# A gated linear attention with an MLP behind it: results kept in 20 buffers and stored by SP, five input buffers, and a new plan

## The chip, the core and the metric

The kernel runs on one core of a Trainium2 chip. The core has five engines that work side by side and wait for each other by semaphores: TensorE (PE in the profile; PEld is its weight load), VectorE (DVE), ScalarE (ACT), GpSimd (POOL) and SyncE (SP). Here SP only issues DMA transfers: loads, transposes and some stores. POOL computes and issues DMA too. Matrix products are written to PSUM, which the kernel uses as six banks and one larger buffer for scores; everything else lies in SBUF.

The metric is the device time of one execution in microseconds, the median of several runs. The difference that can be told from none is about 0.2%.

## What is computed

For 4 batches, 8 heads, 768 steps and head size 48, a state of 48 x 48 per head is decayed by a gate and updated by an outer product; the query reads it. The result, 3072 rows of 384, goes through two matrices with SiLU between them.

```python
f = 1.0 / (1.0 + np.exp(-f_logit))
for t in range(S):
    state = f[:, :, t, :, None] * state + np.einsum('bhd,bhe->bhde', k[:, :, t], v[:, :, t])
    y[:, :, t] = np.einsum('bhd,bhde->bhe', q[:, :, t], state)
...
x = np.ascontiguousarray(attn_out.transpose(0, 2, 1, 3)).reshape(B * S, H * D)
h = x @ w_in                     # 384 -> 2048
g = h * (1.0 / (1.0 + np.exp(-h)))
return (g @ w_out).astype(np.float32)   # 2048 -> 384
```

## The kernel before

The 768 steps are cut into 6 chunks of 128; with 4 batches that makes 24 units. Unit u is chunk u // 4 of batch u % 4, and units 2P and 2P+1 form pair P. Four tiles `f`, `k`, `q`, `v` (128 x 384 in f32) are loaded for each unit.

A unit goes through these tasks, in the names of the planner (`make_tasks`, from L72) and the lines of `emit` (from L467) that carry them out:

- E, L (ACT, L463 and L465): the logarithm of the gate, by exponential and logarithm, for one unit or for a pair at once.
- cs (PE, L511 and L515): its cumulative sum over the chunk. ia, al, a (ACT, L518, L522, L520): exponentials of that sum.
- ki, vb (POOL, L524 and L526): k scaled, v cast to bf16. qg (DVE, L528): q scaled.
- The scaled q and k are transposed, either by PE and a copy (tq L534, qkc L536), or, for the units in `turned`, by one DMA transpose that SP issues (qkD, L538).
- sc (PE, L545): scores. at (DVE, L549): the causal mask. y (PE, L554 and L558): the unit's result. yc (DVE, L562): its copy to bf16.
- d (PE, L576), sd (DVE, L581 or L583), su (POOL, L587): the new state, used by the same batch's next unit, u + 4.
- The result is transposed for the first matrix, by PE and a copy (yT L568, xc L570), or, for the units in `turned_y`, by a DMA transpose (xD, L564).

Then, for each pair (for the first four pairs unit by unit), come mi (PE, L492: products with w_in), si (ACT, L488: SiLU), mo (PE, L502: products with w_out, four tasks for each unit), oc (DVE, L505: the unit's 128 x 384 result to SBUF, tile `o`) and so (L508: its store). A store is issued by POOL, or by SP for units from `late_store` on. The weights come in four parts each: wi (L475) and wo (L478), issued by POOL. On ACT exponentials and SiLU need different function sets, so that a change between them costs a table load (L615).

What runs when is settled before the kernel is emitted. `schedule` (from L196) plays the tasks through with assumed durations and gives each engine the ready task of lowest priority value: `pace` x unit + `rank` of its kind + small offsets. `rel` holds a task back to an earliest time. `keep_*` and `hold_*` rule when ACT changes its function set. Where PE would be idle early on, it adds filler products (L480). The tasks are then emitted in the order of the starts found; that order is each engine's program and, for SP, the order of its one DMA queue. Only the order carries over to the chip: real waits are by semaphores.

`SLOTS` (L47) gives the number of buffers of each kind, and the playing-through decides which task gets which. A task that needs a buffer waits until its last user is done. `f`, `k`, `q`, `v` have six buffers, each for a pair of units, so loads can run 12 units ahead; `o` has four.

PE's order before, at three places that matter below (mi_u_j: unit or pair and part; mo_u_m: unit and part):

```
... sc_3 mi_0_1 mi_1_1 mi_2_1 y_3 d_3 yT_3 mi_0_3 mi_1_3 mi_2_3 mi_3_1 mi_3_3 mi_0_0 mi_1_0 mi_2_0 tq_4 mi_3_0 sc_4 mi_0_2 ...
... y_21 mo_18_0 mo_18_1 mo_18_2 mo_18_3 mo_19_0 mo_19_1 mo_19_2 mi_20.21_0 ...
... y_22 mo_19_3 y_23 mo_20_0 ... mo_21_2 mi_22.23_0 ... mi_22.23_7 mo_21_3 mo_22_0 ... mo_23_3
```

Of the kernel before, what the change touches and what calls it, by code (L numbers as in the profile page):

```python
# [20 lines left out]
PAIRS = UNITS // 2  # L21
NTILES = 16
CFG = dict(
    turned=(11, 12, 13, 14, 15, 16, 17, 18, 19, 20, 21, 22, 23),
    turned_y=(7, 10, 12, 14, 15, 17, 19, 20, 21, 22, 23),
    paired=(),
    single_logs=3,
    single=4,
    late_store=18,
    rank=dict(ldf=-74.11, ldk=306.83, ldq=178.45, ldv=335.15, E=-327.79, cs=2020.94, ia=-759.0, ki=-2046.16, vb=759.95,  # L30
         qg=-1495.72, tq=-1801.69, qkc=-1166.67, sc=-2328.29, at=2478.3, y=-12.62, yc=-690.3, yT=-3037.0, xc=1416.83,
         d=2253.93, sd=-1035.38, su=1438.09, qkD=-1636.38, xD=-2535.0, wi=-1290.0, wo=1188.34, mi=-71.8, si=-1785.07,
         mo=3071.62, oc=5435.06, so=-1357.98),
    extra={},
    rel={"wi_0": 23.54, "wi_1": 17.61, "wi_2": 27.48, "wi_3": 20.24, "wo_0": 29.34, "wo_1": 34.31, "wo_2": 38.63, "wo_3":
         39.74},
    pace=166.65,
    mstep=4.83,
    keep_exp=3000.87,
    keep_silu=2633.26,  # L40
    hold_exp=1.01,
    hold_silu=1.0,
    margin=0.0,
    dm=0.16,
)

SLOTS = dict(f=6, k=6, q=6, v=6, e=2, lf=3, ia=2, qk=5, vb=6, qkT=4, atm=3, yb=3, xT=4, hT=4, sd=2, al=6, o=4,  # L47
             st0=1, st1=1, st2=1, st3=1, bank=6, sc=1)


# [339 lines left out]
def planned(cfg, slots):  # L390

    tasks, T = make_tasks(cfg)
    warm = schedule(tasks, slots, cfg)
    return sorted(tasks + warm, key=lambda t: (t.start, t.idx))
# [3 lines left out]
def kernel(  # L398
# [32 lines left out]
    buf = {}  # L431
    for cls, n in SLOTS.items():
        for s in range(n):
# [12 lines left out]

    tasks = planned(CFG, SLOTS)
    where = {}
# [148 lines left out]
    with tc.manual_schedule():  # L597
# [7 lines left out]
        for cls in ("lf", "qk"):  # L605
            for s in range(SLOTS[cls]):
                nc.vector.memset(buf[cls, s][:, :, :, D:64], 0.0)
# [38 lines left out]
```

## Time and profile before

| | before |
|---|---|
| median of 3 runs | 186.0 us (185.97 to 186.32) |
| the profiled execution | 186.71 us, span of its instructions 184.8 us |
| mean granted TensorE clock | 0.981 |
| busy: PE, ACT, DVE, POOL | 175.7, 126.6, 90.9, 72.2 us |
| stores: by POOL, by SP | 18, 6 of 192 KB each |
| issue to landing, median: POOL's stores, SP's stores | 3.7 us, 1.9 us |
| loads f, k, q, v | 24 each, 192 KB, landing after 3.9 to 4.2 us |

The span runs from the first instruction to the last. A duration from the timeline is one of that execution, so sums are made against its span. Two pages' parts are read together below: what an engine waited for, and the chain that ended last, which goes back from the last instruction to what released each step. Matrix products overlap, so the duration of one product is longer than what it adds to PE's time; the chain's pieces show what it adds.

### The profile page before, as it was taken

To read this page: it belongs to the slowest core of one execution; us is meant where nothing else is said; L and a number is where in the kernel's file an instruction comes from. 1 tells how busy PE (TensorE), PEld (TensorE's weight loads), DVE (VectorE), ACT (ScalarE), POOL (GpSimd) and SP (SyncE) were. 2 spreads that over 40 slices of the span, in tenths; PEclk is the share of its full clock that TensorE was granted. 3 is DMA by queue.
4 is the path that set the end of the run, shared out by engine and by line. 5 is a ranking of instruction groups with operands and counts; after the bars stand their busy time and mean duration, and the time that the engine had idled before them with its cause. 6 is when DMAs were issued, how large, how long until landed. Compare 5 with 4: busy or idle time off the path is not lost.

```text
span 184.8 us, 4961 instructions
## 1 busy us (share of the span) xinstructions
PE 175.7 (95%) x1999; PEld 134.2 (73%) x1999; DVE 90.9 (49%) x178; ACT 126.6 (69%) x216; POOL 72.2 (39%) x122
## 2 busy tenths in 40 slices
PE   7985997999999999999999999999999999999992
PEld 5764777888668787878687678587587776776860
DVE  4185871241476558764914954545365156171021
ACT  5954476554853999899899479698789679550910
POOL 2335648117049418281940853614733616000000
PEclk9998599999999999999999999999999999999999
DMA  6997999999999908999799999799898895704012
GB/s 125 221 208 149 182 224 220 201 175 147 201 198 290 193 21 165 240 199 188 145 178 227 235 174 230 149 228 229 153 242 174 170 212 120 156 4 128 0 44 83
DMA packets 123893, 31.53 MB, mean 171 GB/s; under 512 B 118656, under 2 KB 123008, under 8 KB 123872
## 3 DMA queue, kind: packets, MB, share of 16 engines
q1 hardware_dynamic: 119008, 24.55, 71.6%
q0 software_dynamic: 4864, 6.69, 16.3%
q8 instruction: 15, 0.25, 0.6%
q14 instruction: 6, 0.05, 0.1%
HBM read 25.17 MB, written 4.72 MB: 162 GB/s over the span
## 4 chain that ended last, share of the span: by engine, by line
PE 78%; DMA 7%; SPq 5%; POOL 4%; issue 3%; DVE 0%; POOLq 0%; DVEq 0%
PE bank L502 34%; PE bank L492 31%; SPq L456 5%; DMA w_in_sb<-in_moe_w_in_dram 4%; PE sc L545 3%; DMA k<-in_k_dram 3%; PE bank L558 2%; PE bank L554 2%; PE bank L511 2%; POOL st L587 2%; PE bank L576 2%; PE bank L534 1%; POOL w_in_sb L475 1%; POOL qk L524 1%; PE bank L568 1%
## 5 line engine op out<-in xcount | busy, mean ns | idle before, releaser
L488 ACT ACTIVATE hT<-bank 128x512 bf16<-128x512 f32 x96 | 55.1, 601 | 30.1 <-PE bank L492 27.1
L492 PE MATMUL bank<-xT,w_in_sb 128*128 128x128 bf16 (+1 forms) x768 | 68.9, 246 | 1.1 <-DMA w_in_sb<-in_moe_w_in_dram 0.9
L502 PE MATMUL bank<-w_out_sb,hT 128*128 128x384 bf16 x384 | 69.0, 326 | 0.0
L492 PEld LDWEIGHTS <-w_in_sb 128*128 128x128 bf16 x768 | 58.6, 98 | 8.2 <-DMA w_in_sb<-in_moe_w_in_dram 1.4
L502 PEld LDWEIGHTS <-hT 128*128 128x128 bf16 x384 | 35.5, 98 | 20.4
L549 DVE TENSOR_TENSOR atm<-sc,triu 128x512 bf16<-128x512 f32 x48 | 30.9, 686 | 27.6 <-PE sc L545 27.6
L587 POOL TENSOR_TENSOR st<-sd,al 48x192 bf16<-48x192 f32 x40 | 20.0, 501 | 35.0 <-DVE sd L581 28.5
L524 POOL TENSOR_TENSOR qk<-k,ia 128x384 bf16<-128x384 f32 x24 | 23.8, 999 | 15.3 <-DMA k<-in_k_dram 6.9
L615 ACT ACT_TABLE_LOAD x21 | 26.9, 1283 | 0.4
L505 DVE COPY o<-bank 128x384 f32<-128x384 f32 x24 | 13.3, 555 | 19.6 <-PE bank L502 15.0
L508 POOL DMA_DIRECT2D out_dram<-o x18 | 10.3, 571 | 25.2 <-DVE o L505 25.1
L562 DVE CAST yb<-bank 128x384 bf16<-128x384 f32 x24 | 13.2, 554 | 12.2 <-PE bank L558 7.8
L518 ACT ACTIVATE ia<-bank 128x384 f32<-128x384 f32 x24 | 11.2, 491 | 10.8 <-PE bank L515 6.6
L528 DVE TENSOR_TENSOR qk<-q,bank 128x384 bf16<-128x384 f32 x24 | 13.1, 551 | 11.1 <-ACT bank L520 9.3
L536 DVE COPY qkT<-bank 128x1024 bf16<-128x1024 bf16 x11 | 7.6, 690 | 17.1 <-PE bank L534 17.0
L526 POOL CAST vb<-v 128x384 bf16<-128x384 f32 x24 | 12.1, 506 | 8.5 <-DMA v<-in_v_dram 8.4
L480 PE MATMUL bank<-idle 128*128 128x256 bf16 x72 | 13.4, 339 | 1.1 <-DVE idle L599 1.1
L463 ACT ACTIVATE e<-f 128x768 f32<-128x768 f32 (+1 forms) x15 | 10.7, 713 | 4.1 <-DMA f<-in_f_logit_dram 4.0
L520 ACT ACTIVATE bank<-bank 128x384 f32<-128x384 f32 x24 | 11.6, 489 | 0.3
L545 PE MATMUL sc<-qkT 48*128 48x128 bf16 x192 | 9.8, 222 | 1.4 <-DVE qkT L536 1.3
L465 ACT ACTIVATE lf<-e 128x768 bf16<-128x768 f32 (+1 forms) x15 | 10.7, 716 | 0.4
L545 PEld LDWEIGHTS <-qkT 48*128 48x128 bf16 x192 | 5.5, 95 | 6.4 <-issue 3.7
(35 smaller groups left out, 119.4 us busy)
## 6 DMA issues: line engine op xcount, KB each, us to landing
f<-in_f_logit_dram SPq DMA_DIRECT2D x24, 192.0 KB, 4.0
q<-in_q_dram SPq DMA_DIRECT2D x24, 192.0 KB, 3.9
k<-in_k_dram SPq DMA_DIRECT2D x24, 192.0 KB, 4.2
v<-in_v_dram SPq DMA_DIRECT2D x24, 192.0 KB, 4.1
out_dram<-o POOLq DMA_DIRECT2D x18, 192.0 KB, 3.7
w_in_sb<-in_moe_w_in_dram POOLq DMA_DIRECT2D x4, 384.0 KB, 6.5
w_out_sb<-in_moe_w_out_dram POOLq DMA_DIRECT2D x4, 384.0 KB, 8.6
out_dram<-o SPq DMA_DIRECT2D x6, 192.0 KB, 1.9
```

Of the source, the lines that this page charges most:

```text
L480: return nc.tensor.matmul(at("warm", rest[0])[:, 0:256], idle[:, 0:128], idle, start=True, stop=True)
L488: return nc.scalar.activation(at("hT", P)[:, per * j:per * (j + 1), lo:hi], h, AF.Silu)
L492: nc.tensor.matmul(h[:, i, :], w_in_sb[:, kk, n * 128:(n + 1) * 128], at("xT", P)[:, kk, lo:hi], start=(kk == 0), stop=(kk == KT - 1))
L502: nc.tensor.matmul(o, at("hT", P)[:, n, i * C:(i + 1) * C], w_out_sb[:, n, :], start=(n == 0), stop=(n == NT - 1))
L505: nc.vector.tensor_copy(at("ob", u), at("o", u)[:, 0:d_model])
L524: nc.gpsimd.tensor_mul(at("qk", u)[:, 1, :, 0:D], at("k", P)[:, i], at("ia", u))
L528: nc.vector.tensor_mul(at("qk", u)[:, 0, :, 0:D], at("q", P)[:, i], at("cs", u)[:, 0:HD].rearrange("p (h d) -> p h d", d=D))
L545: nc.tensor.matmul(a_ps[:, r, p, :], qkT[lo:lo + D, 1, p, :], qkT[lo:lo + D, 0, p, :], start=True, stop=True)
L549: nc.vector.tensor_mul(at("atm", u)[:, r], at("sc", u)[:, r], triu[:, None, :].to_broadcast([C, NP, C]))
L562: nc.vector.tensor_copy(at("yb", u), at("y", u)[:, 0:HD])
L587: nc.gpsimd.tensor_mul(at("st", u)[lo:lo + D, :, r * D:(r + 1) * D], at("sd", u)[lo:lo + D, :, r * D:(r + 1) * D], at("al", u)[lo:lo + D, ...
L615: nc.scalar.preload_act_table_set(tables[turn[id(t)]])
```

## The change

The numbers of the planner are replaced, among them which units are transposed by DMA. `late_store=0` gives all 24 stores to SP, and `rel` now names an earliest time for the stores of units 0 to 17. `SLOTS` takes one buffer each from `f`, `k`, `q`, `v` and gives `o` 20 buffers for four. The code that emits the tasks is the same, two lines further down.

```diff
--- before.py
+++ after.py
@@ -21,30 +21,32 @@
 PAIRS = UNITS // 2
 NTILES = 16
 CFG = dict(
-    turned=(11, 12, 13, 14, 15, 16, 17, 18, 19, 20, 21, 22, 23),
-    turned_y=(7, 10, 12, 14, 15, 17, 19, 20, 21, 22, 23),
+    turned=(8, 10, 11, 12, 13, 14, 15, 16, 17, 18, 19, 20, 21, 22, 23),
+    turned_y=(7, 10, 11, 12, 13, 14, 16, 17, 18, 19, 20, 21, 22, 23),
     paired=(),
     single_logs=3,
     single=4,
-    late_store=18,
-    rank=dict(ldf=-74.11, ldk=306.83, ldq=178.45, ldv=335.15, E=-327.79, cs=2020.94, ia=-759.0, ki=-2046.16, vb=759.95,
-         qg=-1495.72, tq=-1801.69, qkc=-1166.67, sc=-2328.29, at=2478.3, y=-12.62, yc=-690.3, yT=-3037.0, xc=1416.83,
-         d=2253.93, sd=-1035.38, su=1438.09, qkD=-1636.38, xD=-2535.0, wi=-1290.0, wo=1188.34, mi=-71.8, si=-1785.07,
-         mo=3071.62, oc=5435.06, so=-1357.98),
+    late_store=0,
+    rank=dict(ldf=-274.93, ldk=-6.43, ldq=-41.44, ldv=84.54, E=-487.94, cs=661.52, ia=25.69, ki=-923.11, vb=746.88,
+         qg=-1254.96, tq=-717.13, qkc=-1681.18, sc=-760.61, at=2386.54, y=201.04, yc=-903.01, yT=-753.16, xc=2561.22,
+         d=816.17, sd=-1700.33, su=-952.45, qkD=-1345.7, xD=-1132.08, wi=808.99, wo=2162.98, mi=187.68, si=-172.94,
+         mo=2099.98, oc=4900.92, so=2468.15),
     extra={},
-    rel={"wi_0": 23.54, "wi_1": 17.61, "wi_2": 27.48, "wi_3": 20.24, "wo_0": 29.34, "wo_1": 34.31, "wo_2": 38.63, "wo_3":
-         39.74},
-    pace=166.65,
-    mstep=4.83,
-    keep_exp=3000.87,
-    keep_silu=2633.26,
-    hold_exp=1.01,
-    hold_silu=1.0,
-    margin=0.0,
-    dm=0.16,
+    rel={"wi_0": 18.84, "wi_1": 18.77, "wi_2": 27.73, "wi_3": 17.67, "wo_0": 28.08, "wo_1": 27.82, "wo_2": 38.93, "wo_3":
+         41.06, "so_0": 154.46, "so_1": 169.69, "so_2": 173.54, "so_3": 134.53, "so_4": 134.8, "so_5": 177.21, "so_6":
+         174.72, "so_7": 167.9, "so_8": 169.39, "so_9": 147.12, "so_10": 123.29, "so_11": 156.38, "so_12": 152.75, "so_13":
+         152.0, "so_14": 161.31, "so_15": 162.52, "so_16": 131.89, "so_17": 155.6},
+    pace=129.78,
+    mstep=6.0,
+    keep_exp=3697.77,
+    keep_silu=3881.14,
+    hold_exp=0.51,
+    hold_silu=0.83,
+    margin=0.01,
+    dm=0.19,
 )
 
-SLOTS = dict(f=6, k=6, q=6, v=6, e=2, lf=3, ia=2, qk=5, vb=6, qkT=4, atm=3, yb=3, xT=4, hT=4, sd=2, al=6, o=4,
+SLOTS = dict(f=5, k=5, q=5, v=5, e=2, lf=3, ia=2, qk=5, vb=6, qkT=4, atm=3, yb=3, xT=4, hT=4, sd=2, al=6, o=20,
              st0=1, st1=1, st2=1, st3=1, bank=6, sc=1)
```

The orders that this gives, where the working speaks of them. POOL early on, before and after (wi_n, wo_n: parts of the weights):

```
before: ki_2 vb_2 wi_1 su_1 ki_3 wi_3 vb_3 su_2 wi_0 su_3 wi_2 wo_0 ki_4 vb_4 wo_1 su_4 wo_2 wo_3 ki_5 ...
after:  ki_2 vb_2 wi_3 su_1 ki_3 wi_0 wi_1 su_2 vb_3 su_3 wi_2 wo_0 wo_1 ki_4 vb_4 su_4 wo_2 wo_3 ki_5 ...
```

PE after, at the same three places as above:

```
... sc_3 mi_0_3 mi_1_3 mi_2_3 y_3 d_3 mi_0_0 yT_3 mi_1_0 mi_2_0 mi_3_0 mi_3_3 mi_0_1 mi_1_1 mi_2_1 tq_4 mi_3_1 sc_4 mi_0_2 ...
... y_20 y_21 mo_17_3 mo_18_0 mo_18_1 mo_18_2 mo_18_3 mo_19_0 sc_22 mo_19_1 mo_19_2 mi_20.21_0 ...
... y_22 y_23 mo_19_3 mo_20_0 ... mo_21_2 mi_22.23_0 ... mi_22.23_7 mo_21_3 mo_22_0 ... mo_23_3
```

SP's queue in the last stage (so_u: a store):

```
before: q_22 qkD_21 k_22 v_22 q_23 k_23 v_23 xD_20 xD_21 qkD_22 so_18 qkD_23 xD_22 xD_23 so_19 ... so_23
after:  q_22 k_22 so_3 v_22 q_23 k_23 v_23 qkD_22 so_4 xD_20 xD_21 qkD_23 so_9 so_10 so_0 so_12 so_13 so_11
        so_16 so_17 so_18 xD_22 xD_23 so_14 so_15 so_19 so_20 so_7 so_8 so_1 so_21 so_2 so_6 so_22 so_5 so_23
```

## The prediction

> **What bounds the kernel now.** I read the share of busy time first, then what PE waited for, then PE's busy time by stretch, and last the chain that ended last and the queues around its weak places.
>
> What PE waited for (engine, line, tile, releaser: total us, times, longest):
>
> ```profile
> PE bank L534 <- POOL qk L524: 1.3, 1, 1.3
> PE sc L545 <- DVE qkT L536: 1.3, 2, 1.1
> PE bank L492 <- DMA w_in_sb<-in_moe_w_in_dram: 0.9, 1, 0.9
> PE bank L568 <- DVE yb L562: 0.5, 1, 0.5
> ```
>
> Busy time of the engines in two long stretches (start:end, length, then busy us and instructions of PE, PEld, DVE, ACT, POOL, then granted clock, DMA share, GB/s):
>
> ```profile
> 60.00:84.00 24.00, 24.00 (x335) 19.16 (x333) 16.16 (x30) 22.59 (x35) 11.45 (x19) 1.00 0.80 158
> 108.00:132.00 24.00, 24.00 (x244) 17.98 (x242) 11.57 (x22) 20.61 (x35) 11.26 (x19) 1.00 1.08 197
> ```
>
> All waits of PE together are some 5 us, all before 36.4 us. From there to the last product at 181.26 us PE never waits, at full granted clock. So there are three terms: when PE becomes dense (36.41 us), the PE work after that (144.85 us), and the tail of 3.5 us to the span's 184.8. What is saved on POOL, DVE, ACT or DMA is worth nothing unless one of these moves.
>
> What makes PE dense at 36.41, in POOL's part of the timeline (start, us; first three lines) and in the chain that ended last (last two):
>
> ```profile
> 22.36 0.81 POOL L475 DMA_DIRECT2D w_in_sb<-in_moe_w_in_dram  x1
> 24.68 0.80 POOL L475 DMA_DIRECT2D w_in_sb<-in_moe_w_in_dram  x1
> 29.27 0.80 POOL L475 DMA_DIRECT2D w_in_sb<-in_moe_w_in_dram  x1
> ...
> 29.27 7.09 DMA w_in_sb<-in_moe_w_in_dram
> 36.41 2.85 PE bank L492 x48
> ```
>
> The four parts of w_in come one by one; the second to fourth issue at the times shown. PE waits 0.94 us for the third (to 32.40), and the fourth, landing at 36.36, starts the dense run.
>
> **The change, part by part.**
>
> PE work. `turned` gains units 8 and 10, so two tasks tq (eight transposes each) leave PE. `turned_y` gains 11, 13, 16 and 18 and loses 15: three tasks yT fewer. Prices from the dense part of the chain:
>
> ```profile
> 55.66 0.17 PE bank L568 x3
> ...
> 71.23 0.45 PE bank L534 x8
> ```
>
> 2 x 0.45 + 3 x 0.17 = 1.41 us less. Nothing covers it, because PE is the bound: −1.41. The products of L492 and L502, of scores, y and d keep their number and shapes; one filler more (73 for 72) lies before the dense run. On DVE two copies L536 (0.69 us) and three L570 (0.35) go too, worth nothing. ACT loses two table loads (19 changes of function set for 21, 1.28 us each), also off the path.
>
> Head. In POOL's new order the second and third parts of w_in follow each other directly, ahead of su_2 and vb_3; the fourth stays behind su_3. So the third issues at about 22.36 + 0.81 = 23.17 instead of 24.68: 1.5 us earlier. The third and fourth landed 36.36 − 32.40 = 4.0 us apart although issued 4.6 apart, which looks like one queue served in turn; then the fourth can land up to 1.5 us earlier too (29.27 + 5.3, the shortest landing of w_in, is 34.6). PE can get back only its own waits there, 0.94 + 0.18 + 0.13 = 1.25 us. The other end: the DMA share in this stretch is 1.2, saturated, so the fourth may land as before: 0. I take −0.9, nearer the gain, since no byte is added and the third is simply asked for earlier. vb_3 moves behind two issues and su_2, to about 25.6 us; y_3 needs it at 26.75, so 1.1 us of cover; if gone, it delays su_3 and the fourth part by as much.
>
> Stores. Eighteen issues leave POOL (0.57 us each, 10.3 us busy, plus the 25.1 us that POOL waited there for results). POOL is busy 39% of the span and PE waits for it nowhere after 36 us: 0. SP now issues all 24, at 0.33 us when the queue is clear. None stands before the last loads, so the saturated DMA (share about 1.0 from 72 to 150 us) carries 18 x 192 KB less while loads run. A gain only if a load was late: 0.
>
> Five input buffers. A load of unit u waits until unit u−10 has been read, instead of u−12. In the trace E of units 16 and 17 starts at 102.32 us, released by its load of 98.64: loads run at most some five units ahead mid-span, less than ten. Early on, unit 10's first load would wait for an exponential that ended long before (at 5.2 us). Cost 0.
>
> More transposes by DMA. SP carries 29 for 24, each 1.2 to 1.3 us to issue, landing 3.5 us (qkT) or 2.6 us (xT) later. Covers in PE's order, summed with the durations above: from a unit's cumulative sum to its scores, for units transposed by DMA, at least 9.5 us after against 8.4 before; from y to its first L492 product, at least 5.0 against 4.55. The old minima ran without a wait. Between: if a transpose lands at its slowest (5.7 us for 3.5) and the cover is used up, 2.2 us each. I take 0, bounds 0 and 4.4 (two such).
>
> Last stage. SP before, from 156 us:
>
> ```profile
> 156.15 1.23 SPq L538 DMA_TRANSPOSE qkT<-qk  x1
> 157.47 0.53 SPq L508 DMA_DIRECT2D out_dram<-o  x1
> 158.09 1.28 SPq L538 DMA_TRANSPOSE qkT<-qk  x1
> 165.28 2.79 SPq L564 DMA_TRANSPOSE xT<-yb  x2
> 168.12 14.14 SPq L508 DMA_DIRECT2D out_dram<-o  x5
> ```
>
> Nine stores now stand between the transposes of unit 23's scores and of unit 22's y, in a gap where SP idled from 159.4 to 165.3. In the new order PE has 11.85 us of work from the end of y_21 to the end of y_23; qkD_23 leaves SP 3.3 us into it and xD_22 is wanted at 12.2, so the nine fit if each takes under 0.99 us. Measured: 0.33 to 0.57 us on SP, and 0.13 x 15 / 3 = 0.65 us of all DMA engines for the last three. Cost 0. The remaining stores lie under 16 us of PE work after that; only so_5 stands between so_22 and the last one, issued about 2 us ahead of it, so the tail keeps its 3.5 us (bounds 0 and +0.65, one store in the way).
>
> Sum: 184.8 − 1.41 − 0.9 = 182.5 of span. The profiled run took 186.71 and the median of the runs is 186.0, 1.2 above the span; so 183.7 us.
>
> The Trainium skill, DMA: Bandwidth & Descriptors, section "Issuing engines are not separate DMA queues", says that issuing from several engines saves only sequencer time, since all share the same DMA engines. By it moving stores to SP brings nothing and costs SP's time, which is how they stand in the sum.
>
> **The rivals.**
>
> Slower, the last stage: in one queue the nine stores hold up xD_22 and xD_23, and the products of units 22 and 23, which start right behind (170.16), wait. For: loads on the same queue took 0.7 to 3 us each while DMA was full. Against: the share there was 0.1 to 0.7. At 1.5 us a store PE idles 9 x (1.5 − 0.99) = 4.6 us: 188.3. It turns the sign from 0.99 + 2.3/9 = 1.25 us a store. The Trainium skill, DMA: Bandwidth & Descriptors, "Queues, rings and completion order", has each DMA engine take one ring's descriptors in order and alternate between rings; by it the stores, formerly on POOL's ring, now precede the transposes. No row shows that collision.
>
> Slower or same, SP mid-span: it issues in order, and a transpose whose input is late holds the loads behind it. xD_7 already kept SP idle from 61.5 to 67.9. One score transpose at 5.7 us with its cover gone gives back 2.2: 185.9; two, 188.1. Against: the covers counted above.
>
> Head not moved, because the weights share a full DMA: only the 1.41 counts, 184.6.
>
> Same, the clock: granted 0.50 from 18 to 24 us, after idle gaps at 13.4 to 17.5. If the new fillers leave it low for 3.4 us more (half the time from 18 to 24, rounded up), the first products lose 1.7: 186.0 − 1.41 + 1.7 = 186.3. The Trainium skill, TensorE: Matmul & The Clock Gate, "What's actually happening", names a free-running window of 3.4 us; the 6 us here agree roughly with two.
>
> **How the numbers follow.** Forecast 0.57 (own range 182.6 to 185.2), head not moved 0.13, clock 0.06, last stage 0.09, SP mid-span 0.15 (0.03 of it within). A measurement here tells 0.2%, 0.37 us, from no change. Faster 0.70, same 0.09, slower 0.21. The range 182.6 to 187.2 leaves out 0.04 below, and above it the last stage with the worse third of SP mid-span, 0.14.
>
> **What would show it.** Right: L534 with 72 and L568 with 30 products; PE dense from about 35.5 us; no wait of PE after; the last product at about 179; stores on SP under 0.7 us each before the xT transposes. Wrong: PE idle at L545 or L492 released by DMA qkT or xT, or by hT; the fourth part of w_in landing at 36.4 or later; a clock below 1 after 24 us; a last store that lands over 2 us after its issue.

## The result and the profile after

| | before | changed |
|---|---|---|
| median of 16 runs each | 186.37 us | 184.90 us |
| ratio to the kernel before, 95% interval | | 0.990 (0.987 to 0.993) |
| the same, second series (10 runs against 27) | | 0.993 (0.989 to 0.996) |
| the profiled execution, its span | 186.71, 184.8 us | 183.91, 182.1 us |
| busy: PE, ACT, DVE, POOL | 175.7, 126.6, 90.9, 72.2 us | 172.7, 124.0, 87.9, 62.3 us |

By the ratios the changed kernel is faster by 1.8 us (1.0%) in the first series and 1.4 us (0.7%) in the second; 183.7 us, 2.3 less than before, was forecast. The ratios leave disturbed runs out, which the medians of the table contain. Their intervals are 0.3 to 0.4% to either side, wider than the 0.2% named at the start, so a term of 0.9 us (0.5%) can only just be told by them. Its profiled execution is one of its shorter ones, so its span shows more, 2.7 us less. Lines of the changed kernel's code stand two higher (L502 is now L504).

What PE waited for in the changed kernel (engine, line, tile, releaser: total us, times, longest):

```profile
PE bank L504 <- DMA w_out_sb<-in_moe_w_out_dram: 1.3, 1, 1.3
PE bank L482 <- DVE idle L601: 1.1, 1, 1.1
PE sc L547 <- DVE qkT L538: 0.8, 3, 0.3
PE bank L560 <- DVE atm L551: 0.7, 2, 0.4
PE bank L513 <- ACT lf L467: 0.6, 1, 0.6
PE bank L494 <- DMA w_in_sb<-in_moe_w_in_dram: 0.3, 1, 0.3
```

The wait for w_in has shrunk to 0.3 us and a new one, for w_out, has come. Busy time in the same two stretches as before (length, then PE, PEld, DVE, ACT, POOL, clock, DMA share, GB/s):

```profile
60.00:84.00 24.00, 24.00 (x323) 18.76 (x320) 14.76 (x29) 21.90 (x37) 10.35 (x17) 1.00 0.82 160
108.00:132.00 24.00, 24.00 (x246) 18.11 (x244) 11.49 (x21) 22.53 (x39) 8.80 (x14) 1.00 0.97 178
```

PE is again busy without a gap, beside less work on POOL. How the dense run begins: POOL's issues of w_in (the first line's second number covers two issues), two lines of PE's timeline (the bracket: idle time before, and its releaser), then the chain that ended last:

```profile
20.51 1.57 POOL L477 DMA_DIRECT2D w_in_sb<-in_moe_w_in_dram  x2
28.24 0.80 POOL L477 DMA_DIRECT2D w_in_sb<-in_moe_w_in_dram  x1
...
33.54 2.85 PE L494 MATMUL bank<-xT,w_in_sb 128*128 128x128 bf16 x48
38.24 1.47 PE L504 MATMUL bank<-w_out_sb,hT 128*128 128x384 bf16 x8 [1.31 <-DMA w_out_sb<-in_moe_w_out_dram]
...
29.04 9.16 DMA w_out_sb<-in_moe_w_out_dram
38.24 1.47 PE bank L504 x8
```

The third part of w_in follows the second at once, as the order said, and no part of w_in ends the wait now: it is the first part of w_out, which took 9.16 us and released PE at 38.24, 1.31 us after PE had nothing else to do. PE is therefore dense from 38.24 us; the prediction had named about 35.5 as a sign of being right. The last stage of SP:

```profile
153.89 1.25 SPq L540 DMA_TRANSPOSE qkT<-qk  x1
155.19 4.54 SPq L510 DMA_DIRECT2D out_dram<-o  x9
162.49 3.26 SPq L566 DMA_TRANSPOSE xT<-yb  x2
165.80 13.68 SPq L510 DMA_DIRECT2D out_dram<-o  x13
```

Nine stores take 4.54 us, 0.50 each, and SP is idle again before the transposes.

To split the span I use two marks that every profile has: the start of the first product with w_out (L502 before, L504 after) and the start of the last copy of a result (L505, L507). Ahead of the first lies the head, between them the dense run. By the two orders PE has the same tasks between the marks in both kernels, except for the two tq and three yT that left.

| profile | first w_out product | dense run | PE idle in it |
|---|---|---|---|
| before | 39.64 | 141.70 | 0 |
| changed | 38.24 | 140.33 | 0 |
| changed, second series | 38.97 | 140.32 | 0 |

From the start of the last copy to the end of the span it is 3.5 us in both kernels.

### The profile page after: what moved, and what is told of

The parts are those of the page before. It is cut to its first block, busy times and chain, and to the rows that moved or that the text cites. A ratio compares the mean times of both kernels' runs of the same rounds, so it can differ in the third digit from the quotient of the medians.

```text
span 182.1 us, 4898 instructions
## 1 busy us (share of the span) xinstructions
PE 172.7 (95%) x1975; PEld 130.2 (72%) x1975; DVE 87.9 (48%) x173; ACT 124.0 (68%) x214; POOL 62.3 (34%) x104
## 4 chain that ended last, share of the span: by engine, by line
PE 77%; SPq 9%; DMA 8%; DVE 2%; issue 1%; POOL 1%; DVEq 0%
PE bank L504 35%; PE bank L494 29%; SPq L458 9%; DMA w_out_sb<-in_moe_w_out_dram 5%; PE sc L547 3%; DMA q<-in_q_dram 3%; PE bank L560 2%; PE bank L556 2%; PE bank L513 2%; PE bank L578 1%; PE bank L536 1%; DVE atm L551 1%; PE bank L517 1%; PE bank L570 1%; POOL st L589 1%
## 5 line engine op out<-in xcount | busy, mean ns | idle before, releaser
L504 PE MATMUL bank<-w_out_sb,hT 128*128 128x384 bf16 x384 | 68.5, 326 | 1.3 <-DMA w_out_sb<-in_moe_w_out_dram 1.3
L504 PEld LDWEIGHTS <-hT 128*128 128x128 bf16 x384 | 35.6, 98 | 22.3 <-DMA w_out_sb<-in_moe_w_out_dram 1.5
L507 DVE COPY o<-bank 128x384 f32<-128x384 f32 x24 | 13.2, 554 | 21.1 <-PE bank L504 21.1
L520 ACT ACTIVATE ia<-bank 128x384 f32<-128x384 f32 x24 | 11.4, 491 | 9.2 <-PE bank L517 4.4
L482 PE MATMUL bank<-idle 128*128 128x256 bf16 x73 | 12.7, 312 | 1.2 <-DVE idle L601 1.1
L538 DVE COPY qkT<-bank 128x1024 bf16<-128x1024 bf16 x9 | 6.2, 688 | 10.7 <-PE bank L536 10.6
L560 PE MATMUL bank<-vb,atm 128*128 128x48 bf16 x192 | 9.2, 183 | 0.7 <-DVE atm L551 0.7
```

What stands on the lines that cost most here:

```text
L504: nc.tensor.matmul(o, at("hT", P)[:, n, i * C:(i + 1) * C], w_out_sb[:, n, :], start=(n == 0), stop=(n == NT - 1))
L507: nc.vector.tensor_copy(at("ob", u), at("o", u)[:, 0:d_model])
```

## The experiments

The edits below are made on the list of planned tasks, between `planned` and the emission. `N` finds a task by name; `move(a, b)` puts a in front of b (behind it with `after=True`). Everything else stays, so the order of all other tasks is the same. Each ratio is against the kernel before, run on the same chip.

**The changed kernel again.**

> The changed kernel once more, beside the three that follow on one chip, so that they can be compared with it. Both theories: about 0.99 of the kernel before. The profile of the change had a span 2.7 us shorter, but the runs' ratio gives only 1.8 us of 186.4; if the head of the span (the start of the dense PE work) varies from run to run, spans and granted clocks of the single runs will show it: runs with a mean clock of 1.0 shorter by 1 us or more than runs at 0.99.

Measured: 0.993 (0.989 to 0.996), median 184.73 us against 186.09. Its runs at a mean clock of 0.995 or more lie between 183.79 and 184.78 us, those below between 184.50 and 185.94; the medians of the two groups are 0.8 us apart. Of the kernel before, 13 runs at 0.995 or more have a median of 186.10, nine between 0.988 and 0.991 one of 185.85, and five at 0.981 or less one of 186.43: no order. So in the changed kernel a lower clock goes with 0.8 us, somewhat less than expected, and in the kernel before with nothing that can be told.

**Six transposes back on PE.**

The edit in words, since its code is long:

```diff
-qkD_8, qkD_10, xD_11, xD_13, xD_16, xD_18    (DMA transposes issued by SP)
+tq, qkc for units 8 and 10                   (PE and a copy on DVE, some four PE tasks ahead of the scores)
+yT, xc for units 11, 13, 16 and 18           (some six PE tasks behind y)
```

> The changed kernel with six of its DMA transposes put back on PE: tq for units 8 and 10, yT for units 11, 13, 16 and 18, each a few PE tasks behind its input. Theory (PE is the bound and its work alone counts): 2 x 0.45 + 4 x 0.17 = 1.58 us slower than the changed kernel, with every microsecond found between the first w_out product and the last. Rival (the DMA transposes cost waits elsewhere that eat what PE saves): no difference, or faster.

Measured: 1.008 (1.004 to 1.012), 2.9 us above the changed kernel by the ratios. The dense run is 143.41 us, 3.09 more. The timeline of PE shows small waits that the changed kernel has not (the bracket: idle time before, and its releaser):

```profile
88.64 0.33 PE L608 MATMUL bank<-ident,yb 128*128 128x128 bf16 x3 [0.21 <-DVE sd L621]
105.88 0.33 PE L608 MATMUL bank<-ident,yb 128*128 128x128 bf16 x3 [0.30 <-DVE o L545]
```

The bracket understates them: a w_out product lasts 0.33 us but adds only 0.16 to PE's time, so the next product can be late before PE counts as idle. Measured from the start of one product to the start of the next, against the usual distance, PE loses 0.16, 0.21, 0.37, 0.47 and 0.28 us ahead of the products at 72.82, 77.95, 88.64, 105.88 and 127.19 us, 1.49 in all, and the chain that ended last passes through DVE at each of the five. With the 1.58 us of PE work that makes 3.07 of the 3.09. So the theory's work is there in full, and as much again is waits for a DVE that now carries six copies more. Where I put the tasks, not only that they are on PE, is part of this price.

**Old stores and old buffers in the new plan.**

```diff
+for u in range(18):
+    move(f"so_{u}", f"oc_{u}", after=True)
+    N[f"so_{u}"].eng = "POOL"
-f=5, k=5, q=5, v=5, o=20
+f=6, k=6, q=6, v=6, o=4
```

The buffers are taken in turn, by unit for the results and by pair for the inputs.

> The changed kernel's plan with the stores and buffers of the kernel before: the stores of units 0 to 17 are issued by POOL right behind their copies, four result buffers, six input buffers. Theory: the same time as the changed kernel within 0.3 us, since PE never waits for POOL, a store or a load after the head. Rival (the gain comes from taking the stores out of the loads' way, and POOL out of their wait): about 1.8 us slower, that is the time of the kernel before.

Measured: 1.012 (1.007 to 1.017), median 188.79 us. The theory fell, by 4 us. The dense run is 144.47 us, with PE idle for 3.21 of it. Four of the waits, from PE's timeline:

```profile
55.61 0.40 PE L556 MATMUL bank<-ident,qk 128*128 128x128 bf16 x4 [0.43 <-POOL qk L546]
96.90 0.81 PE L514 MATMUL bank<-xT,w_in_sb 128*128 128x256 bf16 x6 [0.86 <-ACT hT L510]
98.22 0.40 PE L567 MATMUL sc<-qkT 48*128 48x128 bf16 x8 [0.51 <-DMA qkT<-qk]
133.42 3.44 PE L514 MATMUL bank<-xT,w_in_sb 128*128 128x256 bf16 x30 [0.84 <-DMA xT<-yb]
```

The first is POOL's own order: ki of a unit stood behind three stores, which waited 8.85 us for their copies:

```profile
52.83 1.70 POOL L530 DMA_DIRECT2D out_dram<-o  x3 [8.85 <-DVE o L527]
54.54 1.01 POOL L546 TENSOR_TENSOR qk<-k,ia 128x384 bf16<-128x384 f32 x1
```

In the changed kernel the same ki starts at 50.21, after POOL had been idle for 7.50 us too, there for the exponential al; so the stores made ki some 4 us late, not 8.85. What made the SiLU of the second wait late was not followed up. The last two are DMA transposes that land too late: by the chain that ended last they took 6.03 and 4.38 us, and the second was also issued later, at 127.63 us for 124.30 in the changed kernel. Time from issue to landing of all 15 transposes of q and k, in the changed kernel:

```profile
DMA to landing us min/median/max: 3.1/3.5/5.5
```

and with the stores on POOL:

```profile
DMA to landing us min/median/max: 3.1/4.0/6.0
```

For those of y the median goes from 3.1 to 3.5 us. Half a microsecond is of the size of these waits; how much of the 4 us it accounts for, beside POOL's order, is not shown.

**Stores on POOL, new buffers; and stores on POOL, only the results' buffers old.** The edit of the stores is the same as above; the first keeps 20 result and five input buffers, the second has four result and five input buffers.

> The changed kernel with the stores of units 0 to 17 issued by POOL right behind their copies; its 20 result buffers and five input buffers stay. The run with old stores and old buffers was 4 us slower than the changed kernel, with PE waiting for DMA transposes, for POOL's ki and for SiLU. Theory (the stores are what hurts: they occupy POOL in order and the DMA engines among transposes with little cover): again about 188.8 us, with the same kinds of waits. Rival (the four result buffers or the six input buffers are what hurts): the time of the changed kernel, 184.7.

> The changed kernel with the stores of units 0 to 17 on POOL, four result buffers and five input buffers. With four and six it was 1.012 of the kernel before, with 20 and five 1.027. If the five input buffers cost that difference once stores share POOL and DMA: about 1.027 here. If the 20 result buffers do: about 1.012.

Measured: 1.027 (1.020 to 1.033), median 191.8 us, and 1.016 (1.011 to 1.021). With stores on POOL the new plan is slower than the kernel before whichever of the three sets of buffers it has, so it is the stores there that it cannot bear; with 20 result buffers it lost even more than the theory's 188.8 us. The second one's dense run is 145.29 us with 3.92 us of PE idle; the longest wait is again for a transpose of y:

```profile
133.52 3.44 PE L512 MATMUL bank<-xT,w_in_sb 128*128 128x256 bf16 x30 [1.21 <-DMA xT<-yb]
```

Five input buffers for six change nothing that can be told (1.016 against 1.012, overlapping intervals). That 20 result buffers come out above four is what the second case of the last expectation allows for, but the intervals just touch, the two were not run on the same chip, and a cause was not found: it stays open.

**Late stores and buffers alone, in the plan before.**

```diff
+so_0 ... so_8 behind qkD_23, so_9 ... so_17 behind xD_23, all by SP
-f=6, k=6, q=6, v=6, o=4
+f=5, k=5, q=5, v=5, o=20
```

> The kernel before, its plan and its transposes, with only the stores and buffers changed: all stores by SP, nine ahead of the transposes of units 22 and 23 and the rest behind them, 20 result buffers, five input buffers. Theory (late stores save nothing where PE has no wait to lose; they only make room for more DMA transposes): the kernel before within 0.3 us, and at most the head of a run differs. Rival (taking the stores out of the middle is by itself worth the gain): 1 us faster or more.

Measured: 1.002 (0.998 to 1.006); dense run 141.89 us with no idle of PE, against 141.70. The old plan had no wait that late stores could remove.

**The weights' order alone, and its reverse.**

```diff
+move("wi_0", "wi_3", after=True)      # in the kernel before
```

> The kernel before with one issue moved: the third part of w_in directly behind the second, ahead of vb_3 and su_2, as in the changed kernel. Theory of the prediction: the third part lands up to 1.5 us earlier and PE becomes dense up to 0.9 us earlier, 185.2 us. Rival (the DMA engines are full, and the next thing that PE needs, a load or the first part of w_out, lands as late as before): 186.1, with PE's wait moved to another release.

```diff
+move("wi_1", "su_3")                  # in the changed kernel
```

> The changed kernel with the third part of w_in back behind su_2 and vb_3, as in the kernel before. Prediction's head term: up to 0.9 us slower than the changed kernel. Theory after the run of the kernel before with this order alone (no gain): within 0.4 us of the changed kernel, since the parts share full DMA engines and PE's wait only changes its place.

Measured: 0.998 (0.994 to 1.003) and 0.992 (0.989 to 0.995). Neither can be told from the kernel that it was made from. The first interval reaches down to 0.994, 1.1 us, so alone it does not exclude the 0.9 us of the prediction; the second run is the closer test, and lies between the two series of the changed kernel. In the profile of the first (of an execution of 187.98 us) PE still waits, in two places, 1.21 us for w_in and 0.74 us for w_out:

```profile
29.68 5.53 PE L505 MATMUL bank<-xT,w_in_sb 128*128 128x128 bf16 x96 [1.21 <-DMA w_in_sb<-in_moe_w_in_dram]
49.81 1.46 PE L515 MATMUL bank<-w_out_sb,hT 128*128 128x384 bf16 x8 [0.74 <-DMA w_out_sb<-in_moe_w_out_dram]
```

**More fillers for the clock, in the kernel before.**

```diff
+ten filler products more ahead of sc_1, fourteen ahead of tq_2
```

> The kernel before with 24 more filler products on PE, ten ahead of sc_1 and fourteen ahead of tq_2, where PE sat idle (13.4 to 14.5 and 16.0 to 17.4 us) before the granted clock fell to 0.50 from 18 to 24 us. Theory (part of the change's earlier head is the clock: its profile has 1.00 there, and su_1, ki_3 and the weights' issues come about 1.9 us earlier): the mean clock rises from 0.98 to 1.0 and the time falls by 0.5 to 1 us. Rival (the head waits for loads and weights, not for PE): the clock rises and the time stays.

Measured: 1.006 (1.001 to 1.010), at a clock of 0.999 in the profile. The first w_in product comes at 24.02 us instead of 24.75, the first w_out product at 39.55 instead of 39.64. The clock rose and bought nothing; why it became slower the profile does not show (its span is 185.1).

**Weights earlier still.**

```diff
+for name in ("wi_2", "wo_0"):         # in the changed kernel
+    move(name, "su_3")
```

> The changed kernel with the fourth part of w_in and the first of w_out issued ahead of su_3, in a stretch in which POOL sits idle for 3.5 us (23.8 to 27.2). In the changed kernel PE waits 1.31 us for that part of w_out, issued at 29.04 and landed 9.2 us later. Theory (issue order in the weights' queue sets the landing): issued 3.5 us earlier, it lands before PE wants it, and up to 1.3 us are gained. Rival (the DMA engines are full in this stretch, and what the weights gain the loads of units 4 and 5 lose): less than 0.3 us, with PE waiting for a load's follower instead.

Measured: 0.992 (0.989 to 0.996), no gain on the changed kernel. The profiled execution was a long one (187.69 us) and shows what can happen. On POOL:

```profile
24.38 0.80 POOL L491 DMA_DIRECT2D w_in_sb<-in_moe_w_in_dram  x1
25.18 0.78 POOL L494 DMA_DIRECT2D w_out_sb<-in_moe_w_out_dram  x1
...
35.27 0.99 POOL L540 TENSOR_TENSOR qk<-k,ia 128x384 bf16<-128x384 f32 x1 [5.18 <-DMA k<-in_k_dram]
```

and in the chain that ended last:

```profile
19.59 15.51 DMA k<-in_k_dram
```

The weights go out 4 us earlier, the load of k for unit 4 needs 15.5 us (the median of these loads is 3.8), and PE waits 3.1 us for its follower.

**The same with two loads put behind, and with the first part of w_in earlier.**

```diff
+move("f_6", "v_4", after=True)
+move("f_7", "v_5", after=True)
```

> The run with the fourth part of w_in and the first of w_out ahead of su_3, which gained nothing because the load of k for unit 4 took 15.5 us and PE waited 3.1 us for ki_4; now the gate loads of units 6 and 7, wanted only near 45 us, go behind the loads of units 4 and 5. Theory (the early span is one queue of bytes, and only their order can be chosen): the load of k for unit 4 lands before 32 us, PE's wait for it is gone, and the time is up to 1 us below the changed kernel. Rival (nothing is late by its order, only by the bytes in all): no gain, another wait in its place.

```diff
+move("wi_3", "ki_2")                  # and this, in the next one
```

> As the run before it in this list, and the first part of w_in is issued ahead of ki_2 instead of behind vb_2, about 1.5 us earlier; in a second profile of the changed kernel PE waited 1.8 us for that part. Theory: up to 1 us more. Rival: the loads of k for units 2 and 3 land later by as much, ki_2 and ki_3 too, and nothing is gained.

Measured: 0.990 (0.986 to 0.994), median 184.11 us, the lowest of all; and 1.002 (0.998 to 1.005). In the first the wait for k is gone:

```profile
30.05 0.99 POOL L542 TENSOR_TENSOR qk<-k,ia 128x384 bf16<-128x384 f32 x1
```

and the first w_out product starts at 38.13 us. By its interval it cannot be told from the changed kernel (0.993 beside it in the other series), so it is no more than a candidate. In the second, which asks for the first part 2 us earlier, PE waits in the profile for the gate of unit 5, and the time is back at that of the kernel before:

```profile
22.95 0.48 PE L530 MATMUL bank<-lf,triu 128*128 128x384 bf16 x1 [3.46 <-ACT lf L484]
```

## Why the prediction was right, and where it was not

PE work, −1.41 us: right. The dense run went from 141.70 to 140.33 us, and it is 140.3 to 140.4 in four of the six profiles that keep the new plan from there on (the two of the changed kernel, the third part late, k first). The other two, weights earlier still and the first part earlier too, have 141.18 and 141.28, with idle times of 0.23 us for a transpose and 0.44 for w_out in them. Nothing else of the change shows in the dense run.

Head, −0.9 us: a term was missing, and the size cannot be confirmed. The profiles give −1.40 and −0.67 us; the runs' ratios, 1.8 and 1.4 us, leave 0.4 and 0 for it. The step that failed is "PE can get back only its own waits there", because it counted the parts of w_in alone. They did land earlier: the fourth, issued at 28.24 and landed 5.3 us later, was there at 33.5, for 36.36 before, and no product waited for it. But the first part of w_out stood in no term, although it had little to spare in the kernel before, issued at 30.07, landed 8.8 us later, at 38.9, and wanted at 39.64:

```profile
30.07 0.78 POOL L478 DMA_DIRECT2D w_out_sb<-in_moe_w_out_dram  x1
39.64 1.46 PE L502 MATMUL bank<-w_out_sb,hT 128*128 128x384 bf16 x8
```

In the changed kernel it landed at 38.2, with PE ready at 36.93; in the second series PE waits for it too, 0.32 us. So w_out, not w_in, ends the head, and of 2.7 us by which PE was ready earlier the first profile keeps 1.40. The reason "since no byte is added and the third is simply asked for earlier" is not borne out either: that order alone gave 0.998 in the kernel before, and without it the changed kernel had 0.992. The DMA engines are full there (share 1.2), and in the profiles of the runs that moved weights forward what was asked for earlier made something else late: w_out, k or the gate. What made the head of the changed kernel's profiles a little earlier is not settled.

Stores, 0: right for the sum and wrong as a reason. Alone they are worth nothing (1.002). But the prediction said "A gain only if a load was late" and did not ask what would be late in the new plan: the transposes. With 18 stores on POOL the same plan is 1.012 to 1.027 of the kernel before. In this plan the late stores earn nothing themselves; they let five more transposes move off PE without a wait. No run has the five transposes in a plan made for stores on POOL, so whether another order could have borne both is open. One reading was wrong without effect: a store, so_3, does stand before the last four loads.

More transposes by DMA, 0 with bounds 0 and 4.4: the value held, because the stores were late. The argument, that the smallest covers are not below those that ran without a wait before, was too weak: with the same covers and the stores on POOL the dense run grew by 4.15 and 4.97 us (144.47 and 145.29 for 140.32), about the upper bound or above it, though the waits for ki and for SiLU are in that too. A cover counts only at the landing times of its own surroundings, 3.5 or 4.0 us, and with POOL's order as it stands.

Five input buffers, 0: right as far as the runs can tell. Last stage, 0: right; nine stores at 0.50 us, against the 0.99 at which PE would have waited, and a tail of 3.5 us in both. The rival of stores that hold up xD_22 is refuted. Of it the Trainium skill, DMA: Bandwidth & Descriptors, "Queues, rings and completion order", gave the mechanism, one ring taken in order; here the nine stores, issued from 155.19 us on, had landed by 161.6, before the transposes were issued at 162.49.

The Trainium skill, DMA: Bandwidth & Descriptors, "Issuing engines are not separate DMA queues", holds that issuing from several engines saves only sequencer time, usually small beside the transfer. In this kernel the sequencer's part was not small: POOL's stores waited 8.85 us for copies, and ki behind them came some 4 us late. The runs do not separate this from the DMA traffic among the transposes; both moved with the same edit.

The clock: not the cause. It was 1.00 after and 0.98 before in the profiles, but raising it in the kernel before gave nothing: in the profiles with more fillers and with late stores alone it was 0.999 and 1.000, and the first w_out product came at 39.55 and 39.32 us, for 39.64 at 0.981. (The 3.4 us in that rival are not half of the six from 18 to 24; 3.0 would give 186.1 us.)

## What to carry to other kernels

Where one engine is busy without a gap, count what leaves that engine; the rest of a change can only make that possible or undo it, and an edit that is worth nothing alone can be what the useful one rests on: test it in the new order too, not only in the old. When a wait is to be shortened, look up the landing of the next transfer as well: it may have little to spare. A stretch whose DMA engines are full is an order of bytes: here asking earlier for one transfer made another late, so decide which is wanted last and put that one behind. A cover that was enough once is a statement about the traffic around it.

## What was not expected of the hardware

While POOL's queue moved weights, a 192 KB load on SP's queue took 15.5 us to land in one long execution, and 11.4 in the first profile of the changed kernel, against a median of 3.8 in both. And with 18 stores of 192 KB put among the DMA transposes their median landing rose by only half a microsecond (3.5 to 4.0 and 3.1 to 3.5 us), while the whole, with POOL's waits, became some 4 us longer.
